# Five turns instead of three for the first two token chunks, with the partial sums added in the output by accumulating DMAs

## The chip, the cores and the metric

The kernel runs on one core of one Trainium2 chip. The metric is the device time of one execution in microseconds (us). A core has five engines that this text speaks of: the tensor engine (PE in the profile, its weight loads PEld), the vector engine (DVE), the scalar engine (ACT), GpSimd (POOL) and the sync engine (SP), which here only issues DMAs.

## What is computed

Linear attention with softmaxed queries and keys, and behind it a feed-forward layer with h - tanh(h) as its activation:

```python
q_s = softmax(q, axis=-1)                 # q, k, v: (8 batches, 8 heads, 576 tokens, 64), float32
k_s = softmax(k, axis=2)                  # over the tokens
kv  = einsum('bhsd,bhse->bhde', k_s, v)
x   = einsum('bhsd,bhde->bhse', q_s, kv)  # then as (4608 tokens, 512)
h   = x @ w_in                            # w_in (512, 2048), float64
g   = h - tanh(h)
out = g @ w_out                           # w_out (2048, 512), float64; out in float32
```

## The kernel before

**Chunks and steps.** The 4608 tokens are nine chunks (j) of 512, each of four tiles of 128. The 2048 columns of the hidden layer are 16 slices (f) of 128. One step (j, f) has two products. `h_step` (L493) makes a slice of h, transposed, in 12 matmuls of 128x512 into the tile `ph`; two buffers of `ph` take turns. Each float32 operand is a sum of two float32r parts (`xh`, `xl` of x.T; two parts of each weight), and three of the four partial products are taken, so that four blocks of 128 rows make 12 matmuls. Behind it ACT and DVE work out g: `u`, `t`, `vv`, `m` on ACT (L503 to L511), and on DVE four instructions (L507, L512, L513, L514). ACT rounds g to `gh` (L516), POOL makes the rest `gl` (L519). `o_step` (L533) multiplies g of one step by a slice of w_out, 12 matmuls for the four tiles, into four PSUM banks `po`. It runs LAG = 2 steps behind its `h_step`: PE's order is h(n), o(n-2), h(n+1), o(n-1), and so on.

**Weights.** They come as float64, in 32 pieces of 128x512 (16 of w_in, 16 of w_out; 512 KB each). `load_weight` (L87) issues the DMA on SP, two pieces ahead of the decoding. `split_weight` (L100) decodes a piece into two float32r parts with integer and float work: for a common piece two ACT instructions (L125, L128), three on DVE (L135, L140, L145), one more on ACT (L153) and one on POOL (L154); a third of the pieces (`apart`) has one ACT and one POOL instruction more (L122, L123, L151) and one less on DVE (L132, L145). The intermediate `c` has three buffers in the pool `dec`, tag `c`.

**Preparing a chunk.** `prepare` (L444) makes x of a chunk: for each new batch it loads keys and values, takes the maximum of the keys over the tokens on DVE (`kv_max`) and PE, the exponentials (`kv_sub`: L272 on DVE, L273 on ACT), the products `pk` of keys and values (`kv_mm`, L284), and normed blocks `kvbd` of them (`kv_norm`, L297 to L302). Queries get maximum, difference (POOL, L366), exponential (ACT, L371), sum (DVE, L379) in `q_soft`, their quotient `qn` on POOL (L403) and a transpose `pt` on PE in `q_t`, and `x_mm` (L435) makes `px`, from which ACT and DVE write `xh` and `xl` (L440, L441). Each of these calls is put at a half step: the first half of a step stands behind its h product, the second behind its o product. `half_step` (L669) maps the places of `prepare` to half steps of the whole program, with maps of their own for chunks 1, 2 and 3. From chunk 2 on, the second part of a batch's values goes through the one buffer of tag `v`: POOL's memset (L194) waits until `pk` of the first part has read it, and then SP loads. Queries have one buffer of tag `q`; a load waits for the quotient of the tile before it.

**The order.** PE and SP take their work in program order (`manual_schedule`, L681); on DVE, ACT and POOL the Tile scheduler sets the order. Steps are numbered from 0. Steps 0 to 7 are chunk 0 with slices 0 to 7 (F0 = 8), steps 8 to 23 all of chunk 1, steps 24 to 31 the rest of chunk 0, and from step 32 on chunks 2 to 8 follow in order. At the end of the first turn of chunk 0 (its o product is in step 9) ACT copies the four banks (L555) and SP writes them to a place in DRAM (`aside`, L566); four steps before the end of the second turn they are loaded again (`o_back`), and DVE adds them to the banks (L558), which SP then writes to the output. All other chunks end with four copies (L564), on ACT but for the last chunk's, into the tag `c`, and SP's writes (L569). Four pieces of the weights are decoded ahead of step 0, 13 in steps 0 to 7, and 15 in steps 8 to 19, five in four steps.

Of the kernel before, what the change touches and what calls it, by code (L numbers as in the profile page):

```python
# [19 lines left out]
# h - tanh(h) = h*u*C2*((u + PA)**2 + PB), u = h*h, to float32's last bits for u <= U_MAX.  # L20
U_MAX = 0.04
# (M_SCALE*h)**2 as an integer is 0 up to there.
# [5 lines left out]
# 2**-112 times the largest high word of a float64 that float32 can hold, read as a float32.  # L28
# [4 lines left out]
def attn_moe_kernel(  # L33
# [46 lines left out]
    # A piece of the weights, 128 x 512, arrives as float64 in the place where its two  # L80
    # float32r parts stay.
# [5 lines left out]
    def load_weight(kind: str, f: int):  # L87
        # What the second chunk's attention loads goes ahead of the pieces that can wait.
# [11 lines left out]
    def split_weight(kind: str, f: int, *after):  # L100
        """Decode a piece behind the instructions in after; other work may come at a yield."""
# [14 lines left out]
        # The exponent's eight lowest-order usable bits move into float32's field by a product  # L116
        # with 2**-112 on the word read as a float32 and a shift by three. The low word gives
        # the three bits that are missing: its first three, rounded, where 15/16 keeps them
        # under eight.
# [39 lines left out]
    # Partition p of a pair of tiles has two tokens that follow one another, 2p and 2p + 1.  # L159
# [25 lines left out]
    def v_load(b: int, st: dict, u: int):  # L185
        # A one before the first token's values of a head, and one behind the second's.
# [33 lines left out]
    def kv_max_t(b: int, st: dict):  # L220
# [5 lines left out]
        # In two parts of 12 bits, which hold a float32.  # L226
# [502 lines left out]
```

## Time and profile before

| | |
|---|---|
| time, median of 3 runs | 944.33 us (944.32 to 944.75) |
| span of the profiled execution | 944.0 us, 12627 instructions |
| PE busy | 898.7 us, 95% |
| DVE busy | 637.2 us, 68% |
| ACT busy | 560.6 us, 59% |
| POOL busy | 350.6 us, 37% |
| mean granted TensorE clock | 0.987 |

The span is the time from the first to the last instruction of one profiled execution on its core; it lies 0.3 us under the median of the timed runs. A busy share is the time in which an engine had an instruction running. Rows of the timeline give the start from the beginning of the span, how long the row took, engine, line, operation, the tile written and those read, how many instructions are merged into the row, and, in square brackets, the idle time of that engine just before it and what ended it. Rows of the windows give, for a stretch A:B, its length and then busy time and number of instructions of PE, PEld, DVE, ACT and POOL, the granted clock, the DMA share and GB/s.

### The profile page before, as it was taken

How to read it: one execution, taken by the hardware profiler on the slowest of the kernel's cores; microseconds unless marked ns; L12 is line 12 of the kernel's file. 1: busy time of each engine (PE TensorE's matmuls, PEld its weight loads, DVE VectorE, ACT ScalarE, POOL GpSimd, SP SyncE). 2: the span in 40 equal slices, each digit the busy share in tenths (PEclk: the TensorE clock that was granted, in tenths of full speed). 3: DMA queues.
4: the chain of work that ended last, by engine and by line, in shares of the span. 5: the costliest groups of instructions: out<-in, count | busy, mean ns of one | idle time of the engine just before them, and what ended most of it. 6: DMA issues, size and time to landing. Idle time of an engine off the chain costs nothing.

```text
span 944.0 us, 12627 instructions
## 1 busy us (share of the span) xinstructions
PE 898.7 (95%) x4676; PEld 738.0 (78%) x4676; DVE 637.2 (68%) x906; ACT 560.6 (59%) x976; POOL 350.6 (37%) x288
## 2 busy tenths in 40 slices
PE   6586998899999999999999999999999999999998
PEld 6365776678887888888888888888888888888886
DVE  6899989986658675856585747655765456444544
ACT  3677886765646556645564556545745565556554
POOL 4457576653224432432252224322433223222221
PEclk9888999999999999999999999999999999999999
DMA  9950084003032311150015001040210020001001
GB/s 265 300 193 0 1 286 94 0 23 122 14 96 50 87 37 45 34 123 1 12 57 123 1 1 57 23 101 1 68 45 1 1 68 13 1 1 45 1 1 45
DMA packets 79774, 57.44 MB, mean 61 GB/s; under 512 B 14688, under 2 KB 72032, under 8 KB 79712
## 3 DMA queue, kind: packets, MB, share of 16 engines
q1 hardware_dynamic: 79712, 56.63, 21.5%
q8 instruction: 37, 0.61, 0.3%
q14 instruction: 25, 0.20, 0.1%
HBM read 46.14 MB, written 10.49 MB: 60 GB/s over the span
## 4 chain that ended last, share of the span: by engine, by line
PE 79%; DVE 10%; ACT 4%; issue 4%; DMA 2%; POOL 1%; SPq 1%; DVEq 0%; POOLq 0%; ACTq 0%
PE po L542 36%; PE ph L499 35%; PE px L435 3%; PE pk L284 2%; DMA q<-in_q_dram 2%; PE pt L413 1%; DVE g L513 1%; DVE g L514 1%; DVE t L512 1%; DVE g L507 1%; DVE c_o L140 1%; DVE c_o L145 1%; DVE raw_o L135 1%; ACT gh L516 1%; ACT u L503 1%
## 5 line engine op out<-in xcount | busy, mean ns | idle before, releaser
L542 PE MATMUL po<-w_o,gh 128*128 128x512 f32 x1152 | 361.9, 395 | 0.0
L519 POOL TENSOR_TENSOR gl<-g,gh 128x512 fp32r<-128x512 f32 x143 | 196.2, 1372 | 435.5 <-ACT gh L516 408.0
L499 PE MATMUL ph<-xh,w_i 128*128 128x512 f32 x1152 | 315.0, 395 | 4.3 <-ACT xh L440 2.1
L499 PEld LDWEIGHTS ph<-xh,w_i 128*128 128x128 f32 x1152 | 214.0, 189 | 50.3 <-ACT xh L440 2.8
L507 DVE SCALAR_TENSOR_TENSOR g<-u,ph 128x512 f32<-128x512 f32 x144 | 98.4, 683 | 229.4 <-ACT t L505 227.3
L542 PEld LDWEIGHTS po<-w_o,gh 128*128 128x128 f32 x1152 | 214.7, 189 | 44.6 <-ACT aside L555 0.4
L542 PE MATMUL po<-w_o,gl 128*128 128x512 f32 x576 | 227.1, 394 | 7.4 <-POOL gl L519 7.3
L516 ACT CAST gh<-g 128x512 fp32r<-128x512 f32 x144 | 89.4, 621 | 196.4 <-DVE g L514 189.5
L499 PE MATMUL ph<-xl,w_i 128*128 128x512 f32 x576 | 155.8, 392 | 2.5 <-DVE xl L441 2.5
L503 ACT ACTIVATE u<-ph 128x512 f32<-128x512 f32 x144 | 85.8, 596 | 93.5 <-PE ph L499 93.1
L513 DVE SCALAR_TENSOR_TENSOR g<-vv,g 128x512 f32<-128x512 f32 x144 | 121.2, 842 | 22.7 <-ACT vv L509 12.5
L542 PEld LDWEIGHTS po<-w_o,gl 128*128 128x128 f32 x576 | 108.6, 189 | 34.6 <-POOL gl L519 10.8
L499 PEld LDWEIGHTS ph<-xl,w_i 128*128 128x128 f32 x576 | 108.6, 189 | 27.0 <-DVE xl L441 3.4
L514 DVE COPY_PREDICATED g<-m,t 128x512 f32<-128x512 int32 x144 | 118.6, 823 | 3.4
L509 ACT ACTIVATE vv<-u,b_pa 128x512 f32<-128x512 f32 x144 | 104.9, 728 | 1.7 <-DVE g L513 1.7
L511 ACT ACTIVATE m<-ph 128x512 int32<-128x512 f32 x144 | 86.5, 601 | 21.3 <-DVE g L507 21.0
L512 DVE TENSOR_TENSOR t<-ph,t 128x512 f32<-128x512 f32 x144 | 98.0, 681 | 1.4 <-ACT m L511 1.1
L505 ACT ACTIVATE t<-ph 128x512 f32<-128x512 f32 x144 | 85.3, 592 | 0.0
L435 PE MATMUL px<-qs,kvbd 128*128 128x128 f32 (+1 forms) x304 | 41.0, 281 | 8.7 <-DVE kvbd L302 7.1
L435 PEld LDWEIGHTS px<-qs,kvbd 128*128 128x128 f32 x304 | 39.3, 195 | 12.7 <-ACT t L505 7.5
L366 POOL TENSOR_TENSOR q<-q,mq 128x1024 f32<-128x1024 f32 x15 | 30.0, 2003 | 37.5 <-DVE mq L365 37.4
L403 POOL TENSOR_TENSOR qn<-q,sq 128x512 f32<-128x512 f32 x30 | 33.6, 1120 | 18.3 <-DVE sq L381 18.1
(101 smaller groups left out, 637.7 us busy)
## 6 DMA issues: line engine op xcount, KB each, us to landing
k<-in_k_dram SPq DMA_DIRECT2D x16, 512.0 KB, 5.6
raw_i<-in_moe_w_in_dram SPq DMA_DIRECT2D x16, 512.0 KB, 8.3
raw_o<-in_moe_w_out_dram SPq DMA_DIRECT2D x16, 512.0 KB, 9.7
q<-in_q_dram SPq DMA_DIRECT2D x15, 512.0 KB, 4.3
v<-in_v_dram SPq DMA_DIRECT2D x14, 512.0 KB, 5.8
out_dram<-o SPq DMA_DIRECT2D x28, 256.0 KB, 2.0
kr<-in_k_dram SPq DMA_DIRECT2D x8, 128.0 KB, 6.3
spare_v<-in_v_dram SPq DMA_DIRECT2D x2, 512.0 KB, 7.8
```

The costliest lines, as they stand in the source:

```text
L435: nc.tensor.matmul(px[:, a, p0:p1], kvbd[b % 2][:, a, :], qs[:, a, p0:p1], start=True, stop=True)
L499: nc.tensor.matmul(ph, w[:, i, c], x[:, c, :], start=(n == 0), stop=(n == len(ops) - 1))
L503: nc.scalar.activation(u, ph, AF.Square)
L507: nc.vector.scalar_tensor_tensor(g, u, C2, ph, op0=ALU.mult, op1=ALU.mult)
L509: nc.scalar.activation(vv, u, AF.Square, bias=b_pa)
L511: last = nc.scalar.activation(m, ph, AF.Square, scale=M_SCALE)
L512: nc.vector.tensor_tensor(t, ph, t, op=ALU.subtract)
L513: nc.vector.scalar_tensor_tensor(g, vv, PB, g, op0=ALU.add, op1=ALU.mult)
L514: nc.vector.copy_predicated(g, m, t)
L516: nc.scalar.copy(gh, g)
L519: eng.tensor_tensor(gl, g, gh.bitcast(F32), op=ALU.subtract)
L542: nc.tensor.matmul(po[t], g[:, cols], wt["o", f][:, w], start=(begin and n == 0), stop=(end and n == 2),)
```

## The change

The first two chunks take the weights in five turns instead of three: steps 0 to 3 are chunk 0 with slices 0 to 3, steps 4 to 11 chunk 1 with slices 0 to 7, steps 12 to 19 chunk 0 with 4 to 11, steps 20 to 27 chunk 1 with 8 to 15, steps 28 to 31 chunk 0 with 12 to 15. From step 32 on the steps are as before. Five pieces of the weights are decoded in steps 0 to 3, and then one in each step, from 4 to 26. Chunk 1 is prepared in steps 0 to 3 instead of 0 to 7, and chunk 2's tiles are spread over the half steps from 55 on, seven for every 17 places of `prepare`, instead of from 48 on, 12 for every 15. `kv_norm` stands ahead of the first product that reads its blocks.

Each turn ends with ACT's copies of the four banks into the tag `c` (20 copies for the two chunks, where there were eight, and four additions on DVE). The first turn of a chunk is written to the output by SP. The sums of a later turn are added to what stands in the output by a DMA with `accum_op=ALU.add`, issued by POOL: twelve such DMAs of 256 KB, four each for the turns that end with steps 19, 27 and 31. `aside`, `o_back` and the additions are gone.

```diff
-        for b in new:
-            put(km + 3, lambda: kv_norm(b, st))
...
+            if new & {b for b, _, _ in batches(i)} and not normed:
+                normed = True
+                put(km + 3, lambda: kv_norm(b, st))
             put(at, lambda i=i: x_mm(i))
...
-    def o_step(j: int, f: int):
+    def o_step(n: int):
+        j, f = steps[n]
         gh, gl = gs.pop((j, f))
-        begin = f == 0 or (j == 0 and f == F0)
-        end = f == NF - 1 or (j == 0 and f == F0 - 1)
+        begin = n == 0 or steps[n - 1] != (j, f - 1)
+        end = n == len(steps) - 1 or steps[n + 1] != (j, f + 1)
...
-            if j == 0 and f < NF - 1:
-                if t % 2 == 0:
-                    both = ap.tile([P, 2, DM], F32, name=f"aside{t}", tag="k", bufs=NKP)
-                o = both[:, t % 2]
-                nc.scalar.copy(o, po[t])
-            elif j == 0:
-                o = back[t // 2][:, t % 2]
-                nc.vector.tensor_tensor(o, po[t], o, op=ALU.add)
-            elif j == NCH - 1 and t % 2:
+            if j == NCH - 1 and t % 2:
                 o = gp.tile([P, DM], F32, name=f"o{j}_{f}_{t}", tag="g")
                 nc.vector.tensor_copy(o, po[t])
             else:
                 o = dec.tile([P, DM], F32, name=f"o{j}_{f}_{t}", tag="c")
                 nc.scalar.copy(o, po[t])
-            if f < NF - 1:
-                nc.sync.dma_start(aside[t], o)
-            else:
-                for rows, p0, p1 in rows_of(out, j * TPC + t):
+            for rows, p0, p1 in rows_of(out, j * TPC + t):
+                if (j, t) in written:
+                    nc.gpsimd.dma_start(rows, o[p0:p1], accum_op=ALU.add)
+                else:
                     nc.sync.dma_start(rows, o[p0:p1])
+            written.add((j, t))
...
-    F0 = 8
-    BACK = 4
-    steps = [(0, f) for f in range(F0)] + [(1, f) for f in range(NF)]
-    steps += [(0, f) for f in range(F0, NF)]
+    turns = [(0, 0, 4), (1, 0, 8), (0, 4, 12), (1, 8, 16), (0, 12, 16)]
+    steps = [(j, f) for j, f0, f1 in turns for f in range(f0, f1)]
+    F0 = turns[0][2]
+    BOTH = len(steps)
...
-            begin = 2 * (NF + F0)
-            return begin - 9 + at if at < 9 else begin + (at - 9) * 12 // 15
+            begin = 2 * (BOTH - turns[-1][2] + turns[-1][1]) - 1
+            return begin - 9 + at if at < 9 else begin + (at - 9) * 7 // 17
...
-            elif n < F0 + SPREAD:
-                pieces_upto(THEN + -(-(len(pieces) - THEN) * (n + 1 - F0) // SPREAD), last)
-            if n == 2 * NF - BACK:
-                o_back()
+            elif split < len(pieces):
+                pieces_upto(split + 1, last)
```

Three places show how the order moves. The first is PE behind the products `pk` of batch 1's keys and values; `pt` are transposed queries and `px` the products that give chunk 1's x. Before, from the second `pk` on:

```order
L284 MATMUL pk_574<-spare_v_431,k_1_416 64x65 x16
L284 MATMUL pk_574<-vr_423,kr_418 64x65 x8
L413 MATMUL pt_690<-ident,qn_688 128x128 x4
L499 MATMUL ph_4_704<-xh_289,w_i_499 128x512 x4
L499 MATMUL ph_4_704<-xl_290,w_i_499 128x512 x4
L499 MATMUL ph_4_704<-xh_289,w_i_499 128x512 x4
L435 MATMUL px_759<-qs_695,kvbd_94 128x128 x4
L542 MATMUL po_0_0_558<-w_o_488,gh_2_543 128x512 x2
```

And PE of the changed kernel from the same `pk` on (its lines are numbered otherwise: L501 is the h product, L535 the o product):

```order
L284 MATMUL pk_503<-spare_v_454,k_1_413 64x65 x16
L284 MATMUL pk_503<-vr_420,kr_415 64x65 x8
L413 MATMUL pt_554<-ident,qn_552 128x128 x4
L435 MATMUL px_570<-qs_559,kvbd_94 128x128 x4
L413 MATMUL pt_579<-ident,qn_577 128x128 x4
L501 MATMUL ph_2_594<-xh_286,w_i_354 128x512 x4
L501 MATMUL ph_2_594<-xl_287,w_i_354 128x512 x4
L501 MATMUL ph_2_594<-xh_286,w_i_354 128x512 x4
L435 MATMUL px_635<-qs_584,kvbd_94 128x128 x4
L413 MATMUL pt_644<-ident,qn_642 128x128 x4
L535 MATMUL po_0_0_651<-w_o_343,gh_0_385 128x512 x2
```

The first `px` stood behind the h product of step 4 and stands now ahead of that of step 2, and the four tiles take one half step each instead of one step each.

The second place is PE at the products `pk` of batch 2's keys and values, in chunk 0's last turn, before:

```order
L284 MATMUL pk_2015<-v_0_1697,k_0_1691 64x65 x16
L542 MATMUL po_0_0_1174<-w_o_1676,gh_15_1906 128x512 x2
L542 MATMUL po_0_0_1174<-w_o_1676,gl_15_1908 128x512
L542 MATMUL po_0_1_1178<-w_o_1676,gh_15_1906 128x512 x2
L542 MATMUL po_0_1_1178<-w_o_1676,gl_15_1908 128x512
L542 MATMUL po_0_2_1182<-w_o_1676,gh_15_1906 128x512 x2
L542 MATMUL po_0_2_1182<-w_o_1676,gl_15_1908 128x512
L542 MATMUL po_0_3_1186<-w_o_1676,gh_15_1906 128x512 x2
L542 MATMUL po_0_3_1186<-w_o_1676,gl_15_1908 128x512
L499 MATMUL ph_10_2059<-xh_289,w_i_1108 128x512 x4
L499 MATMUL ph_10_2059<-xl_290,w_i_1108 128x512 x4
L499 MATMUL ph_10_2059<-xh_289,w_i_1108 128x512 x4
```

Behind these rows the second `pk` follows, which reads `v_1`. In the changed kernel:

```order
L284 MATMUL pk_2172<-v_0_1852,k_0_1846 64x65 x16
L535 MATMUL po_8_0_1789<-w_o_1989,gh_14_2043 128x512 x2
L535 MATMUL po_8_0_1789<-w_o_1989,gl_14_2045 128x512
L535 MATMUL po_8_1_1793<-w_o_1989,gh_14_2043 128x512 x2
L535 MATMUL po_8_1_1793<-w_o_1989,gl_14_2045 128x512
L535 MATMUL po_8_2_1797<-w_o_1989,gh_14_2043 128x512 x2
L535 MATMUL po_8_2_1797<-w_o_1989,gl_14_2045 128x512
L535 MATMUL po_8_3_1801<-w_o_1989,gh_14_2043 128x512 x2
L535 MATMUL po_8_3_1801<-w_o_1989,gl_14_2045 128x512
L284 MATMUL pk_2172<-v_1_2189,k_1_1848 64x65 x16
L284 MATMUL pk_2172<-vr_1855,kr_1850 64x65 x8
L413 MATMUL pt_2230<-ident,qn_2228 128x128 x4
```

Between the two `pk` stood an o and an h product; now there is the o product alone.

The third place is ACT in step 33, at the end of chunk 0's last turn. Before, no copy stood there, since DVE added the banks:

```order
L503 ACTIVATE u_1_2463<-ph_1_2450 128x512
L505 ACTIVATE t_1_2465<-ph_1_2450 128x512
L509 ACTIVATE vv_1_2469<-u_1_2463,b_pa 128x512
L511 ACTIVATE m_1_2471<-ph_1_2450 128x512
L503 ACTIVATE u_2_2513<-ph_2_2500 128x512
```

In the changed kernel:

```order
L507 ACTIVATE t_1_2492<-ph_1_2477 128x512
L549 COPY o_15_0_2510<-po_12_0_2370 128x512
L511 ACTIVATE vv_1_2496<-u_1_2490,b_pa 128x512
L549 COPY o_15_1_2516<-po_12_1_2374 128x512
L513 ACTIVATE m_1_2498<-ph_1_2477 128x512
L549 COPY o_15_2_2522<-po_12_2_2378 128x512
L549 COPY o_15_3_2528<-po_12_3_2382 128x512
L518 CAST gh_1_2503<-g_1_2494 128x512
L505 ACTIVATE u_2_2544<-ph_2_2531 128x512
```

Four copies stand among the work on g. The tag `c` has three buffers, so the fourth copy waits for the accumulating DMA of the first, and `gh` of step 33 is queued behind it.

More of the change, by code (lines that the diff above doesn't have):

```diff
@@ L476, in prepare @@
             put(km + 3, lambda: kv_mm(b, st, NKP))
-        unit = None
+        unit, normed = None, False
         for i, at in when.items():
@@ L484, in prepare @@
             put(at - 3, lambda i=i: q_t(i))
+            if new & {b for b, _, _ in batches(i)} and not normed:
+                normed = True
+                put(km + 3, lambda: kv_norm(b, st))
             put(at, lambda i=i: x_mm(i))
-        for b in new:
-            put(km + 3, lambda: kv_norm(b, st))
     gs = {}
     po = {}
+    written = set()
     def h_step(j: int, f: int):
@@ L521, in h_step @@
         return last
-    dram = ctx.enter_context(tc.tile_pool(name="dram", bufs=1, space=bass.MemoryType.DRAM))
-    aside = dram.tile([TPC, P, DM], F32, name="aside")
-    back = []
-    def o_back():
-        for n in range(2):
-            t = ap.tile([P, 2, DM], F32, name=f"back{n}", tag="k", bufs=NKP)
-            nc.sync.dma_start(t, aside[2 * n : 2 * n + 2].rearrange("t p m -> p t m"))
-            back.append(t)
-    def o_step(j: int, f: int):
+    def o_step(n: int):
+        j, f = steps[n]
         gh, gl = gs.pop((j, f))
-        begin = f == 0 or (j == 0 and f == F0)
-        end = f == NF - 1 or (j == 0 and f == F0 - 1)
+        begin = n == 0 or steps[n - 1] != (j, f - 1)
+        end = n == len(steps) - 1 or steps[n + 1] != (j, f + 1)
         for t in range(TPC):
@@ L540, in o_step @@
             cols = slice(t * P, (t + 1) * P)
-            for n, (g, w) in enumerate(((gh, 0), (gh, 1), (gl, 0))):
+            for m, (g, w) in enumerate(((gh, 0), (gh, 1), (gl, 0))):
                 nc.tensor.matmul(
@@ L545, in o_step @@
                     wt["o", f][:, w],
-                    start=(begin and n == 0),
-                    stop=(end and n == 2),
+                    start=(begin and m == 0),
+                    stop=(end and m == 2),
                 )
@@ L564, in o_step @@
                 nc.scalar.copy(o, po[t])
-            if f < NF - 1:
-                nc.sync.dma_start(aside[t], o)
-            else:
-                for rows, p0, p1 in rows_of(out, j * TPC + t):
+            for rows, p0, p1 in rows_of(out, j * TPC + t):
+                if (j, t) in written:
+                    nc.gpsimd.dma_start(rows, o[p0:p1], accum_op=ALU.add)
+                else:
                     nc.sync.dma_start(rows, o[p0:p1])
+            written.add((j, t))
     LAG = 2
-    F0 = 8
-    BACK = 4
-    steps = [(0, f) for f in range(F0)] + [(1, f) for f in range(NF)]
-    steps += [(0, f) for f in range(F0, NF)]
+    turns = [(0, 0, 4), (1, 0, 8), (0, 4, 12), (1, 8, 16), (0, 12, 16)]
+    steps = [(j, f) for j, f0, f1 in turns for f in range(f0, f1)]
+    F0 = turns[0][2]
+    BOTH = len(steps)
     steps += [(j, f) for j in range(2, NCH) for f in range(NF)]
-    FIRST, THEN, SPREAD = 4, 2 * F0 + 1, 12
+    FIRST, THEN = 4, 2 * F0 + 1
     APART = range(6, 2 * NF, 3)
@@ L685, in attn_moe_kernel @@
                 pieces_upto(FIRST + -(-(THEN - FIRST) * (n + 1) // F0), last)
-            elif n < F0 + SPREAD:
-                pieces_upto(THEN + -(-(len(pieces) - THEN) * (n + 1 - F0) // SPREAD), last)
-            if n == 2 * NF - BACK:
-                o_back()
+            elif split < len(pieces):
+                pieces_upto(split + 1, last)
             for half in range(2):
                 if half and n >= LAG:
-                    o_step(*steps[n - LAG])
+                    o_step(n - LAG)
                 for call in calls.pop(2 * n + half, ()):
@@ L695, in attn_moe_kernel @@
         for n in range(len(steps) - LAG, len(steps)):
-            o_step(*steps[n])
+            o_step(n)
 _INS = ["q", "k", "v", "moe_w_in", "moe_w_out"]
```

## The prediction

> **What bounds the kernel now.** I read the slices of the page first, then the windows by stage, then PE's timeline. In the slices (23.6 us each) PE is short of full in the first nine, and there DVE is the fullest engine:
>
> ```profile
> PE   6586998899999999999999999999999999999998
> ...
> DVE  6899989986658675856585747655765456444544
> ...
> PEclk9888999999999999999999999999999999999999
> ```
>
> PE's timeline gives the first h products of steps 0, 8, 24, 32 and 33, and of steps 128 and 143 in the last chunk:
>
> ```profile
> 31.04 1.19 PE L499 MATMUL ph<-xh,w_i 128*128 128x512 f32 x4 [1.67 <-ACT xh L440]
> ...
> 78.75 2.05 PE L435 MATMUL px<-qs,kvbd 128*128 128x128 f32 x8 [7.12 <-DVE kvbd L302]
> ...
> 106.88 1.21 PE L499 MATMUL ph<-xh,w_i 128*128 128x512 f32 x4 [0.47 <-ACT xh L440]
> ...
> 210.85 1.07 PE L499 MATMUL ph<-xh,w_i 128*128 128x512 f32 x4
> ...
> 263.61 1.08 PE L499 MATMUL ph<-xh,w_i 128*128 128x512 f32 x4
> ...
> 269.08 1.08 PE L499 MATMUL ph<-xh,w_i 128*128 128x512 f32 x4
> ...
> 848.02 1.08 PE L499 MATMUL ph<-xh,w_i 128*128 128x512 f32 x4
> ...
> 930.08 1.08 PE L499 MATMUL ph<-xh,w_i 128*128 128x512 f32 x4
> ```
>
> A step of PE work alone is 269.08 - 263.61 = 5.47 us, 2.74 for each product. A chunk is (848.02 - 263.61) / 6 = 97.4, so preparing one costs PE 97.4 - 16 x 5.47 = 9.9. From step 0 to step 32 there are 32 h products, 30 o products and two preparations: 62 x 2.735 + 19.8 = 189.4 us of work, and it took 263.61 - 31.04 = 232.6. So 43 us are lost there, and all the change does lies there. The windows say to whom (columns: stretch, length, busy us and instructions of PE, PEld, DVE, ACT, POOL, clock):
>
> ```profile
> 37.77:106.88 69.11, 51.00 (x289) 40.07 (x287) 67.21 (x84) 50.41 (x89) 43.19 (x31) 0.88 0.33 114
> 106.88:210.85 103.97, 94.34 (x394) 73.44 (x395) 94.98 (x123) 78.64 (x142) 67.38 (x44) 0.98 0.31 91
> 140.00:180.00 40.00, 34.47 (x138) 26.29 (x138) 39.67 (x52) 29.96 (x55) 25.70 (x16) 0.96 0.33 71
> 210.85:263.61 52.76, 52.76 (x325) 44.10 (x324) 32.78 (x51) 31.17 (x55) 17.15 (x17) 1.00 0.19 61
> ```
>
> DVE is busy 67.21 of 69.11 us until step 8 and 39.67 of 40.00 in the worst of the decoding, and then 20 us idle in the last eight steps, where PE runs full. So DVE bounds the first 200 us, and idles where its work is gone. Part of its time is not its own: the same instruction takes 1.76 us beside POOL's and 0.68 without:
>
> ```profile
> 69.16 1.76 DVE L140 SCALAR_TENSOR_TENSOR c_o<-raw_o 128x512 uint32<-128x512 uint32 x1
> ...
> 96.48 0.68 DVE L140 SCALAR_TENSOR_TENSOR c_i<-raw_i 128x512 uint32<-128x512 uint32 x1
> ...
> 68.60 1.77 POOL L154 TENSOR_TENSOR w_i<-c_i,w_i 128x512 fp32r<-128x512 f32 x1
> ```
>
> **The change part by part.** DVE's work from 37.77 (its first instruction on g, with the same order ahead of it in both kernels) to step 32 is 67.21 + 94.98 + 32.78 = 195.0 us. The change takes none of it away; by its order four instructions for batch 3's maximum come ahead of step 32, 4 x 0.80 = 3.2, which makes 198.2. What changes is where DVE has to wait.
>
> *Steps 0 to 3.* Ahead of chunk 1's first h product stand 48 DVE instructions from 37.77 on, where before 84 started in that stretch. At 67.21 / 84 = 0.80 us each that is 38.4. Twice DVE must wait for PE, since h of steps 2 and 3 now stands behind a `px`: a transpose (0.35), h (2.74) and two ACT instructions (0.6 each) less the copies of x that DVE and ACT do meanwhile (0.6 and 0.7), 3.0, and much the same for step 3, 2.5. So step 4 starts at 37.77 + 38.4 + 5.5 = 81.7. If POOL disturbs less it is 79, if the waits add up 85. By then PE has done 4 h, 2 o and a preparation, 26.3 us of work; before, that much was done at about 86. The 7.12 us wait for `kvbd` goes; what is late next is h of step 2 behind `px`.
>
> *Steps 4 to 27.* What is left for DVE is 198.2 - 38.4 less the 32 instructions that stand in steps 28 to 31 at 32.78 / 51 = 0.64, 20.6: 139.2 us. PE needs 24 x 5.47 and about a third of a preparation, 3.4: 134.7. One piece a step makes the two nearly equal, so neither runs far ahead. DVE's idle share here lies between that of the densest stretch, 0.33 of 40 us, and that of steps 8 to 23, 9.0 of 104. I take 2%, since DVE stays the longer one: 2.8 (0 to 12). DVE is done with step 27 at 81.7 + 139.2 + 2.8 = 223.7. PE is about level with it: in the decoding a step's last DVE instruction ends 4.5 us behind its h product (160.85 to 165.36),
>
> ```profile
> 160.85 0.61 PE L542 MATMUL po<-w_o,gh 128*128 128x512 f32 x2
> ...
> 164.62 0.74 DVE L514 COPY_PREDICATED g<-m,t 128x512 f32<-128x512 int32 x1
> ```
>
> and PE does an o product and a `px` meanwhile, 4.2. Step 28 starts at 223.4.
>
> *Steps 28 to 31.* Here chunk 2's tiles are pressed from eight steps into four. PE's work is 21.9 + 9.9 - 3.4 = 28.4. Three chains no longer fit beside it. Their links before:
>
> ```profile
> 220.93 1.15 PE L284 MATMUL pk<-v,k 128*64 128x65 f32 x32
> ...
> 222.63 0.12 POOL L194 MEMSET v<- 128x16 f32 x1
> 222.78 0.38 SPq L196 DMA_DIRECT2D v<-in_v_dram  x1
> ...
> 227.68 1.15 PE L284 MATMUL pk<-v,k 128*64 128x65 f32 x32
> 228.76 0.68 PE L284 MATMUL pk<-vr,kr 64*64 64x65 f32 x16
> ...
> 230.65 0.40 SPq L351 DMA_DIRECT2D q<-in_q_dram  x1
> ...
> 232.72 0.86 DVE L302 TENSOR_TENSOR kvbd<-pk,rs 64x256 f32<-64x256 f32 x2
> ...
> 234.97 1.22 DVE L365 TENSOR_REDUCE mq<-q 128x16 f32<-128x1024 f32 x1 [1.40 <-DMA q<-in_q_dram]
> ...
> 242.80 1.05 POOL L403 TENSOR_TENSOR qn<-q,sq 128x512 f32<-128x512 f32 x1 [4.57 <-DVE sq L381]
> ```
>
> The second `pk` waits for values loaded only when the first `pk` has been read: memset, issue and a lone load of 4.3 us (230.65 to 234.97, where DVE waited for it), 4.6 in all. An o and an h product hid it; now there is one of 2.74. That leaves 1.9, and up to 3 more when the memset stands behind a late `gl` on POOL: 3.0. Then `px` waits for `kvbd`, 4.2 us behind the last `pk` (229.4 to 233.6), beside 3.1 of PE work: 1.1. And the quotient for the last tile came 15.0 us behind the second `pk` (228.8 to 243.85); PE's work up to its transpose is 11.3 and the 1.1 just counted: 2.6 more. Sum 28.4 + 6.7 = 35.1: step 32 at 258.5.
>
> *Ends of turns.* Copies on ACT are more by 12 x 0.6, hidden, since ACT is busy 78.64 of 104. Where decoding goes on they stand among ACT's work as `aside` did, whose copies came over four microseconds and cost PE nothing to speak of (0.08 us over its usual pace):
>
> ```profile
> 119.47 0.58 ACT L555 COPY aside<-po 128x512 f32<-128x512 f32 x1
> ...
> 123.63 0.61 ACT L555 COPY aside<-po 128x512 f32<-128x512 f32 x1
> ...
> 124.29 0.73 PE L542 MATMUL po<-w_o,gh 128*128 128x512 f32 x2
> ```
>
> No row shows an accumulating DMA or POOL's issue of one. It must read what it adds to and then write, so it costs at least a write, 2.0 us, and, with all else in its way, up to the longest median here, 9.7:
>
> ```profile
> raw_o<-in_moe_w_out_dram SPq DMA_DIRECT2D x16, 512.0 KB, 9.7
> ...
> out_dram<-o SPq DMA_DIRECT2D x28, 256.0 KB, 2.0
> ...
> q_rest<-in_q_dram SPq DMA_DIRECT2D x8, 128.0 KB, 3.1
> ```
>
> I take a read and a write in turn, 3.1 + 2.0 = 5.1, and 1 us for the issue (POOL's shortest row of this size above is 1.05). In step 33 the first copy ends 1.3 us behind h; 6.1 us later the fourth copy may start, and is done at 7.9. PE wants that bank at 2.74 + 2.74 + 2.06 = 7.5: 0.4 lost. At the end of the turn of step 19 the third copy waits in the same way, some 1.5 us beyond PE's need, half of it hidden behind DVE; at that of step 27 two preparation products more cover it. Together 1.2. POOL's gl is queued behind these issues, with over 4 us until o reads it.
>
> The Trainium skill, "DMA: Bandwidth & Descriptors" (section "Anatomy of one DMA — SWDGE (gpsimd) path"), fits a GpSimd-issued transfer as 2.0 us and its bytes at 436 GB/s, which for 256 KB would be 2.6 us by estimate, for plain copies. By that the 1.2 us of this term would be nothing, and the forecast 939.2. No run here shows such a transfer yet.
>
> **The sum.** Step 32 moves from 263.6 to 258.5, and 1.2 is lost behind that: a gain of 3.9 us on a span of 944.0. Beyond step 33 the order is the same. The span is 0.3 under the median, so the time is 944.3 - 3.9 = 940.4.
>
> **The rivals.** *DVE stays full* (0.2): PE falls behind nowhere, DVE idles 1% in steps 4 to 27 and the loads come early enough. Then only its gaps count, 4 in the first steps, 1.4, and 9 in the last four: 37.77 + 198.2 + 14.4 = 250.4, a gain of 13 and 931. For it speaks 39.67 of 40.00; against it that two engines with equal work never fit without gaps.
>
> *The gain is given back* (0.17): the first turn saves its 4 us, and the chains of steps 28 to 31 take 10 to 11 instead of 6.7, for instance because `gl` of step 27 comes 3 us late and the clock falls after the wait, as it did around the 7.12 us wait (the 0.88 of that window). Then 944.3 within 1.9 us, which is 0.2%, about what the measurement can tell from no change.
>
> *Slower, by the accumulating DMAs* (0.21): ACT stands still before the third or fourth copy, and behind it wait `gh`, and so `gl` and PE. The price is one for one beyond what the cover allows at each of three ends; from about 7 us a transfer instead of 5.1, 2 us at each end and in all 6, nothing is left of the 3.9 and it turns to loss. At the bound of 9.7 us it is 4.6 at each, 14 in all, some of it hidden: 950. For it speaks that three banks of `c` serve four copies; against it the 2.0 us of a write. The Trainium skill, in the same page, section "SWDGE vs HWDGE vs iDMA", says that GpSimd writes the descriptors into SBUF, where DVE can lock it out. That would lengthen the issue where DVE is busiest, and work for this rival; no run here shows it yet.
>
> **How the numbers follow.** Forecast (935 to 942.4) 0.42, more gain 0.2, no difference 0.17, slower 0.21. Faster by over 0.2% is 0.42 + 0.2 = 0.62. The low end takes in the DVE rival, 931. The high end takes the accumulating rival up to its middle, 949, and leaves the worst of it and an even shorter first part outside.
>
> **What would show it.** Right: step 4 at 79 to 85 us without a long wait for `kvbd`; DVE over 95% from there to about 220, with PE waits for `gl` of less than a microsecond; waits of PE ahead of the second `pk` of batch 2 and of the last tile's transpose, 2 to 5 us each; step 32 at 254 to 263; accumulating DMAs that land in 4 to 7 us. Wrong: PE waits for `po` banks at the ends of turns, ACT idle ahead of a copy for a DMA, or DVE idle by more than a tenth in steps 4 to 27.

## The result and the profile after

The changed kernel takes 955.0 us in the median of four runs (953.57 to 956.11), against 944.54 for the kernel before on the same chip (944.32 to 944.79). The ratio is 1.0111, with a 95% interval of 1.0097 to 1.0126: about 10.5 us slower, where 3.9 us less was forecast. Each run takes 1.8 us more than its span; the profiled one has a span of 953.5, against 944.0 before.

The same three slices of the page as before (23.6 to 23.8 us each):

```profile
PE   7579999889799999999999999999999999999998
...
DVE  6967777869556675767575757755766547544544
...
PEclk9679999889999999999999999999999999999999
```

PE is at nine tenths or more in slices 4 to 7, where before it had 6, 9, 9 and 8, while DVE is at seven tenths there (before, eight and nine). Then PE drops in slices 8, 9 and 11, and the clock in 8 and 9 too. PE's timeline says when steps 0, 4, 20, 28 and 32 begin:

```profile
30.67 1.19 PE L501 MATMUL ph<-xh,w_i 128*128 128x512 f32 x4 [1.67 <-ACT xh L440]
...
79.80 1.10 PE L501 MATMUL ph<-xh,w_i 128*128 128x512 f32 x4
...
172.93 1.07 PE L501 MATMUL ph<-xh,w_i 128*128 128x512 f32 x4
...
235.43 1.18 PE L501 MATMUL ph<-xh,w_i 128*128 128x512 f32 x4
...
274.35 1.08 PE L501 MATMUL ph<-xh,w_i 128*128 128x512 f32 x4
```

Before, steps 20, 28 and 32 began at 184.2, 238.9 and 263.6. So the changed kernel is 11.2 us ahead at step 20, 3.4 ahead at step 28 and 10.7 behind at step 32. It gets 1.2 back at step 38 and keeps 9.5 to the end. The windows between these points (columns as before):

```profile
30.67:79.80 49.13, 34.69 (x213) 28.44 (x214) 37.98 (x58) 30.19 (x52) 22.98 (x19) 0.72 0.32 94
79.80:172.93 93.13, 89.01 (x386) 71.70 (x384) 73.09 (x107) 75.09 (x138) 50.53 (x35) 1.00 0.51 151
172.93:235.43 62.50, 53.69 (x219) 41.51 (x218) 51.43 (x68) 44.32 (x79) 39.91 (x29) 0.92 0.19 37
235.43:274.35 38.92, 32.61 (x215) 26.99 (x214) 24.22 (x39) 18.95 (x34) 15.68 (x16) 0.91 0.47 102
```

In steps 4 to 19 PE works 89.0 of 93.1 us and DVE only 73.1. DVE waits there for PE's products, by way of ACT's `t`, which reads them. This is the instruction that opens each step's work on g, with its count, busy us, mean ns, idle us before it and what ended that:

```profile
L509 DVE SCALAR_TENSOR_TENSOR g<-u,ph 128x512 f32<-128x512 f32 x15 | 10.3, 687 | 15.2 <-ACT t L507 13.6 <-POOL c_o L151 1.6
```

So PE is the bound there. Where the lead goes again, the timelines show three kinds of wait. The first are copies at the ends of turns (in steps 6 and 22; 1.9 us more in step 14):

```profile
97.30 0.74 PE L535 MATMUL po<-w_o,gh 128*128 128x512 f32 x2 [2.11 <-ACT o L549]
...
198.24 0.59 ACT L549 COPY o<-po 128x512 f32<-128x512 f32 x1 [0.97 <-DMA out_dram<-o]
...
198.87 0.94 PE L535 MATMUL po<-w_o,gh 128*128 128x512 f32 x2 [2.50 <-ACT o L549]
```

The second kind comes around step 20. The rest of the queries is issued only at 167.5 us, behind ten weight pieces and a batch's keys and values, which themselves follow the writes of an end of a turn on SP, and it lands late; DVE waits, POOL waits for DVE with `gl` behind it, and PE for `gl`. One step on, PE waits for a piece that is decoded just in time:

```profile
167.54 1.27 SPq L340 DMA_DIRECT2D q_rest<-in_q_dram  x2
...
174.63 0.69 DVE L365 TENSOR_REDUCE mq_rest<-q_rest 128x8 f32<-128x512 f32 x1 [1.77 <-DMA q_rest<-in_q_dram]
...
175.39 1.43 POOL L366 TENSOR_TENSOR q_rest<-q_rest,mq_rest 128x512 f32<-128x512 f32 x1 [5.22 <-DVE mq_rest L365]
...
178.56 0.66 PE L535 MATMUL po<-w_o,gl 128*128 128x512 f32 x1 [1.10 <-POOL gl L521]
...
187.90 0.50 PE L535 MATMUL po<-w_o,gh 128*128 128x512 f32 x1 [1.22 <-POOL w_o L154]
```

The third kind stands in steps 28 to 31: the lone loads of values and queries, and the quotient for the last tile. (The profile calls what ended the first of these waits "issue"; that it is the load of values is shown below, where the load is left out and the wait goes.)

```profile
246.41 1.52 PE L284 MATMUL pk<-v,k 128*64 128x65 f32 x32 [3.94 <-issue]
...
254.36 1.22 DVE L365 TENSOR_REDUCE mq<-q 128x16 f32<-128x1024 f32 x1 [3.86 <-DMA q<-in_q_dram]
...
263.11 0.66 PE L413 MATMUL pt<-ident,qn 128*128 128x128 f32 x4 [2.36 <-POOL qn L403]
```

And the operation that no row of before showed, POOL's accumulating DMA (duration of an issue, then landing, min/median/max):

```profile
L553 POOL DMA_DIRECT2D out_dram<-o x12: 856/891/1531, 193.7 to 289.8; - x12
...
DMA to landing us min/median/max: 3.7/4.6/6.2
```

Eight of these twelve belong to the turns that end with steps 27 and 31, and PE waits for no copy at either end.

### The profile page after: what moved, and what is told of

Its sections match the earlier page's. It is cut to its first block, busy times and chain, and to the rows that moved or that the text cites. A ratio compares the mean times of both kernels' runs of the same rounds, so it can differ in the third digit from the quotient of the medians.

```text
span 953.5 us, 12685 instructions
## 1 busy us (share of the span) xinstructions
PE 906.4 (95%) x4676; PEld 746.7 (78%) x4676; DVE 618.2 (65%) x902; ACT 567.0 (59%) x988; POOL 354.4 (37%) x300
## 4 chain that ended last, share of the span: by engine, by line
PE 80%; DVE 7%; DMA 4%; ACT 4%; issue 3%; POOL 1%; SPq 0%; DVEq 0%; ACTq 0%; POOLq 0%
PE po L535 36%; PE ph L501 36%; PE px L435 3%; PE pk L284 2%; PE pt L413 2%; DMA k<-in_k_dram 1%; DMA q<-in_q_dram 1%; DVE t L514 1%; DVE g L515 1%; DVE g L516 1%; DMA q_rest<-in_q_dram 1%; ACT u L505 1%; ACT gh L518 1%; ACT vv L511 1%; DVE g L509 1%
## 5 line engine op out<-in xcount | busy, mean ns | idle before, releaser
L535 PE MATMUL po<-w_o,gh 128*128 128x512 f32 x1152 | 364.6, 398 | 9.6 <-ACT o L549 6.7
L501 PE MATMUL ph<-xh,w_i 128*128 128x512 f32 x1152 | 317.0, 397 | 1.7 <-ACT xh L440 1.7
L535 PEld LDWEIGHTS po<-w_o,gh 128*128 128x128 f32 x1152 | 215.5, 190 | 58.3 <-ACT o L549 10.1
L509 DVE SCALAR_TENSOR_TENSOR g<-u,ph 128x512 f32<-128x512 f32 x144 | 98.6, 685 | 248.1 <-ACT t L507 244.4
L501 PEld LDWEIGHTS ph<-xh,w_i 128*128 128x128 f32 x1152 | 216.9, 191 | 46.8 <-ACT xh L440 1.9
L535 PE MATMUL po<-w_o,gl 128*128 128x512 f32 x576 | 227.7, 395 | 1.6 <-POOL gl L521 1.6
L501 PE MATMUL ph<-xl,w_i 128*128 128x512 f32 x576 | 156.8, 394 | 1.1 <-DVE xl L441 1.1
L515 DVE SCALAR_TENSOR_TENSOR g<-vv,g 128x512 f32<-128x512 f32 x144 | 118.4, 822 | 23.4 <-ACT vv L511 12.4
L535 PEld LDWEIGHTS po<-w_o,gl 128*128 128x128 f32 x576 | 109.3, 190 | 26.7 <-POOL gl L521 2.4
L501 PEld LDWEIGHTS ph<-xl,w_i 128*128 128x128 f32 x576 | 109.4, 190 | 25.5 <-DVE xl L441 1.6
L516 DVE COPY_PREDICATED g<-m,t 128x512 f32<-128x512 int32 x144 | 116.3, 808 | 3.3
L514 DVE TENSOR_TENSOR t<-ph,t 128x512 f32<-128x512 f32 x144 | 98.1, 681 | 3.2 <-ACT m L513 2.6
L435 PEld LDWEIGHTS px<-qs,kvbd 128*128 128x128 f32 x304 | 39.4, 195 | 7.2 <-issue 3.2
```

Source lines behind the costliest of these rows:

```text
L435: nc.tensor.matmul(px[:, a, p0:p1], kvbd[b % 2][:, a, :], qs[:, a, p0:p1], start=True, stop=True)
L501: nc.tensor.matmul(ph, w[:, i, c], x[:, c, :], start=(n == 0), stop=(n == len(ops) - 1))
L509: nc.vector.scalar_tensor_tensor(g, u, C2, ph, op0=ALU.mult, op1=ALU.mult)
L514: nc.vector.tensor_tensor(t, ph, t, op=ALU.subtract)
L515: nc.vector.scalar_tensor_tensor(g, vv, PB, g, op0=ALU.add, op1=ALU.mult)
L516: nc.vector.copy_predicated(g, m, t)
```

## The experiments

Each experiment was forecast before it ran, and five theories were set against each other. **A**: the order of turns leaves chunk 2's preparation four steps. **B**: the accumulating DMAs cost by themselves. **C**: chunk 2's first loads stand behind the writes of a turn's end on SP's queue and come late. **D**: the copies wait for places that they share with the decoding. **E**: DVE's work is bunched in steps 20 to 28 and takes any lead of PE back. Ratios are against the kernel before on the same chip, with their intervals. For the main ones, the starts of steps in the profiled execution:

| kernel | median us | ratio (95%) | step 20 | step 28 | step 32 |
|---|---|---|---|---|---|
| before | 944.5 | 1 | 184.2 | 238.9 | 263.6 |
| changed | 955.0 | 1.0111 (1.0097 to 1.0126) | 172.9 | 235.4 | 274.4 |
| e9: copies in weight places | 948.45 | 1.0037 (1.0023 to 1.0052) | 170.2 | 228.2 | 267.6 |
| e14: e9 without the lone loads | 941.23 | 0.9960 (0.9946 to 0.9974) | 171.0 | 231.0 | 260.2 |
| e17: e9, lone loads earlier | 944.75 | 1.0011 (1.0002 to 1.0019) | 170.4 | 230.1 | 263.5 |
| e12: eight steps last, loads early | 944.03 | 0.9995 (0.9986 to 1.0005) | 179.1 | 238.0 | 263.3 |
| e15: three turns, twelve steps last | 957.67 | 1.0142 (1.0127 to 1.0157) | 197.0 | 254.2 | 276.9 |

### Turns, transfers and loads, one at a time

The first experiment (e1) changes the order of turns and the pace of decoding, and takes chunk 2's spacing from before:

```
-    turns = [(0, 0, 4), (1, 0, 8), (0, 4, 12), (1, 8, 16), (0, 12, 16)]
+    turns = [(0, 0, 4), (1, 0, 8), (0, 4, 8), (1, 8, 16), (0, 8, 16)]
+    FIRST, THEN, SPREAD = 4, 2 * F0 + 1, 20
-                pieces_upto(split + 1, last)
+                pieces_upto(min(len(pieces), THEN + -(-(len(pieces) - THEN) * (n + 1 - F0) // SPREAD)), last)
-            begin = 2 * (BOTH - turns[-1][2] + turns[-1][1]) - 1
+            begin = 2 * (BOTH - turns[-1][2] + turns[-1][1])
```

> Third turn cut to four steps and last turn lengthened to eight (chunk 0 f4-7, chunk 1 f8-15, chunk 0 f8-15), the 23 pieces left spread over 20 steps, chunk 2's tiles at the old spacing over eight steps. All twelve accumulating DMAs stay. Theory A (the order of turns: chunk 1 ends with step 27, so chunk 2's preparation gets four steps where it had eight, and PE stands there): step 4 at 79.8 as measured, 20 steps of 5.47 and some 6 us of ends of turns until step 24 at 195, then 53 us as before from step 24 to 32: step 32 at 248 to 252, time 930 to 934. Theory B (the accumulating DMAs hold the copies and PE at each end): the three ends stay, 950 or more. Theory C (chunk 2's first loads come late because they stand behind the writes on SP's queue): the loads still stand behind them, 940 to 950.

It took 954.27 us (1.0102, 1.0087 to 1.0117). A missed and B's number was met, and PE's timeline says why: the waits for copies had grown to 17 us. The two longest stand behind the third end, in step 18:

```profile
174.16 1.22 PE L535 MATMUL po<-w_o,gh 128*128 128x512 f32 x2 [2.79 <-ACT o L549]
182.55 1.22 PE L535 MATMUL po<-w_o,gh 128*128 128x512 f32 x2 [6.75 <-ACT o L549]
```

The second (e2) takes the old order of turns with the sums added in the output, so that only how and where the sums are kept differs from before (and `kv_norm`'s place):

```
+    turns = [(0, 0, 8), (1, 0, 16), (0, 8, 16)]
+    FIRST, THEN, SPREAD = 4, 2 * F0 + 1, 12
```

> The old order of turns (eight steps, sixteen, eight) and the old pace of decoding, with the sums added in the output by four accumulating DMAs instead of aside, back and the additions on VectorE. Theory A: as before but for the loads back and the additions, whose step before took 7.5 us against 6.3 in the changed kernel: 942 to 944. Theory B: the four accumulating DMAs cost some 2 to 5 us at their end: 946 to 949. Theory C: 944, as before.

947.28 us (1.0028, 1.0016 to 1.0040), slower than before and within B's range. But B's place is wrong: its accumulating DMAs come at step 33, and PE waits at the end of the first turn, which SP writes with plain DMAs:

```profile
122.56 0.73 PE L535 MATMUL po<-w_o,gh 128*128 128x512 f32 x2 [1.95 <-ACT o L549]
126.12 1.22 PE L535 MATMUL po<-w_o,gh 128*128 128x512 f32 x2 [2.59 <-ACT o L549]
```

This gave theory D. At the same place before, the copies stood in tag `k` and PE lost nothing.

The third (e3) puts chunk 2's first loads ahead on SP's queue:

```
+            if at == 0:
+                return 24
```

> The changed kernel with chunk 2's first loads (keys, first values, the rest of the queries) put at step 12, ahead of the write of the second turn's end on SP's queue. Theory C: VectorE no longer waits 1.8 us for the queries and GpSimd 5 us behind it, steps 20 to 22 take 11 us instead of 19, time 946 to 949. Theories A and B: those steps lose as much to the decoding itself, 953 to 955.

952.62 us (1.0082, 1.0058 to 1.0105), between the two expectations, with an interval that overlaps the changed kernel's. Steps 20 and 21 became full steps, but step 20 began 4.5 us later than in the changed kernel (177.5 against 172.9), with chunk 2's maximum now among the decoding, and step 22 took 11.3 us, with PE waiting 3.4 for a copy: other waits took over.

The fourth (e4) takes the accumulating DMAs out:

```
-                    nc.gpsimd.dma_start(rows, o[p0:p1], accum_op=ALU.add)
+                    pass
```

> The changed kernel with the twelve accumulating DMAs left out (so three of the five partial sums never reach the output). Theory B: with no transfer to wait for, the ends of turns cost nothing and the time is 942 to 946. Theory A: only the 2.7 us that PE waits for copies at step 22 and what the clock loses behind it go, 950 to 953. Theory C: 953 to 955.

949.41 us (1.0045, 1.0028 to 1.0062), 5.6 us less than the changed kernel. The time lies below A's range and above B's. That alone cannot tell the transfer from the place it holds, since without it a copy's place is free at once.

### The copies' places

The edit for the next three puts the copies of the first three ends where before had `aside`:

```
+                if n < 20:
+                    if t % 2 == 0:
+                        both = ap.tile([P, 2, DM], F32, name=f"o{j}_{f}_{t}", tag="k", bufs=NKP)
+                    o = both[:, t % 2]
+                else:
                     o = dec.tile([P, DM], F32, name=f"o{j}_{f}_{t}", tag="c")
```

> The changed kernel with the copies of the first three ends of turns in the four places of tag k (where the kernel before had aside), not in the three of c that the decoding uses too; all twelve accumulating DMAs stay. Theory D (the copies wait for places that they share with the decoding, and the transfers only for as long as they hold such a place): PE's waits for copies (6.4 us at three ends) and the clock lost behind them go, 944 to 948, as without the DMAs or below. Theory B (the accumulating DMAs themselves, their issue on GpSimd and their traffic): only the two ends that write gain, 951 to 953.

> The order of turns of the first experiment (last turn of eight steps) and the copies of the first three ends in tag k. Theories A and D together: the 16 us that PE waited for copies there go, step 32 at 250 to 256, time 931 to 937. If the last turn's length is worth nothing (A falls): as the changed kernel with tag k, 944 to 948. Theory B: 945 to 952, since eight of the transfers still come while PE needs the banks.

> The old order of turns with the sums added in the output (second experiment), and the copies of the end during decoding in tag k, as the kernel before had them. Theory D: PE's 4.5 us of waits at that end go, 942 to 944. Theory B: no change from the second experiment, 946 to 948, because there the accumulating transfers come only at the last end.

The old order of turns (e7) took 943.39 us (0.9985, 0.9976 to 0.9995), 3.9 us less than the second experiment by this edit alone: D held, with plain writes and no accumulating DMA near. The changed kernel with `k` (e5) took 952.81 (1.0084, 1.0064 to 1.0104) and the other order (e6) 949.51 (1.0049, 1.0032 to 1.0066): D's numbers were missed in both, and B's met. Yet PE's waits for copies were down to 0.7 and 3.6 us, but the places in `k` are those of chunk 2's keys, whose load now stood behind the transfers, and DVE waited for it in front of its work on g, 2.7 us in e5. In e6, in step 19:

```profile
177.47 0.69 DVE L213 TENSOR_TENSOR km<-k 128x512 f32<-128x512 f32 x1 [6.61 <-DMA k<-in_k_dram]
```

So the edit had its own fault, and B was not yet out. The cleaner test takes other places: those of the two `w_out` pieces that are loaded last (e9; e11 with the first experiment's turns, e10 and e12 with the third's early loads as well).

```
+                if n < 20:
+                    if t % 2 == 0:
+                        tag = f"wo{NF - 1 - t // 2}"
+                        both = wts.tile([P, 2, DM], F32, name=f"o{j}_{f}_{t}", tag=tag)
+                    o = both[:, t % 2]
```

> The changed kernel with the copies of the first three ends of turns in the places of two weight pieces that are loaded last (o pieces 14 and 15): nothing else uses these places then, neither the decoding nor chunk 2's keys, which VectorE had to wait for in the variant with tag k. Theory D (places): PE's 6.4 us at the three ends go and no new wait for keys comes, step 20 near 169, step 24 near 196, 944 to 948. Theory E (VectorE's work for decoding and chunk 2 is bunched in steps 20 to 28, and the last turn is too short; a lead of PE is taken back there): step 24 near 196, but step 32 at 271 to 273 as in the other variants, 950 to 953.

> The same, and chunk 2's first loads at step 12. Theories C and D together: 941 to 945. Theory E: step 28 gains, the four steps behind it cost 37 to 42 us still: 947 to 951.

> The last turn of eight steps, and the copies of the first three ends in those weight places. Theories A and D: no wait for copies, none of 6.6 us for keys: step 24 at 203 to 208, step 32 at 256 to 261, 937 to 942. Theory E without its part on the last turn (VectorE bunched): step 24 at 212 to 218, step 32 at 266 to 271, 946 to 950.

> The same, and chunk 2's first loads at step 12, so that VectorE can take chunk 2's maxima early. Theories A, C and D: step 24 at 198 to 204, step 32 at 252 to 257, 932 to 938. Theory E: 943 to 948.

e9: 948.45 us, 6.5 less than the changed kernel, with all twelve accumulating DMAs in it, between D's range and E's and 0.45 from D's. The lead at step 20 is D's, and E is right that most of it is gone again by step 32. Its windows of steps 4 to 19, 20 to 27 and 28 to 31:

```profile
79.50:170.20 90.70, 88.71 (x385) 71.67 (x383) 76.04 (x107) 74.08 (x138) 52.45 (x35) 1.00 0.50 151
170.20:228.20 58.00, 50.42 (x218) 39.75 (x219) 52.60 (x69) 43.85 (x79) 43.51 (x29) 0.97 0.21 46
228.20:267.60 39.40, 32.68 (x215) 27.21 (x215) 24.45 (x39) 19.11 (x34) 15.67 (x16) 0.91 0.47 100
```

The early loads added nothing to it (e10: 950.11 us, 1.0053, 1.0034 to 1.0073, within E's range; C falls there). With eight steps for the last turn they did: e11 took 949.11 (1.0044, 1.0029 to 1.0059) and e12, with the loads early, 944.03, level with before, both in E's ranges of time. In e12 the last eight steps run at PE's pace, as A says, but A's time is missed, since steps 4 to 23 take 128.7 us in place of e9's 119.5:

```profile
208.50:263.30 54.80, 53.36 (x326) 44.05 (x325) 38.54 (x56) 31.61 (x59) 25.74 (x23) 1.00 0.36 73
```

Then the accumulating DMAs once more, out of e9 (e13):

> The variant with the copies in weight places (948.5 us), and the twelve accumulating DMAs left out (three of five partial sums never reach the output). Theory B (the transfers cost by themselves: GpSimd's 0.9 us issues, their traffic): 943 to 946. Theory D (they cost only by the places they hold): 947 to 949.

946.86 us (1.0024, 1.0012 to 1.0036). That is 1.6 us less than e9, between the two expectations, and the intervals overlap: theory B's price lies between nothing and some 3 us for all twelve.

### The short last turn

One lone load out of the changed kernel (e8; the first tile of values serves twice):

```
     def v_load(b: int, st: dict, u: int):
+        if b == 2 and u == 1:
+            return
...
+        if b == 2 and u == 0:
+            st["v", 1] = vt
```

> The changed kernel without the load of batch 2's second half of values (the first half is used twice, so that batch's result is another). It prices the lone load in the short last turn: PE's 3.9 us ahead of the second pk and what the clock loses behind it. If that wait is on the path: 949 to 951. If the chains behind it (the quotient for the last tile) end late anyway: 953 to 955.

953.61 us (1.0093, 1.0078 to 1.0109). PE's wait ahead of the second `pk` went, but the one for the last tile's quotient grew from 2.36 to 4.48 us: two chains side by side, and one alone is worth 1.4. So both were taken out of e9 (e14), the load in `q_load` likewise:

```
     def q_soft(unit):
+        if unit == (2, 1):
+            qs_of[unit] = qs_of[2, 0]
+            return
```

> The variant with the copies in weight places, without the load of batch 2's second half of values and without load, maximum, exponential and sum of its second half of queries (the first halves are used twice there). If the two lone loads and the chain behind the second make the last turn long: PE's waits of 3.9 and 2.8 us, VectorE's 4.0 us for the queries and the clock lost behind them go, steps 28 to 32 in 29 to 32 us instead of 39.4, time 938 to 942. If it is PE's clock or the work itself: 945 to 948.

941.23 us (0.9960, 0.9946 to 0.9974), 7.2 us under e9: steps 28 to 31 in 29.2 us, PE busy throughout at full clock. This takes out work too (DVE has 19.0 us in that stretch instead of 24.4), so 7.2 us is an upper bound for the price of the waits.

```profile
230.97:260.20 29.23, 29.23 (x215) 24.46 (x214) 18.97 (x34) 17.76 (x33) 13.63 (x14) 1.00 0.52 100
```

With all work left in, the loads can only be issued earlier. In e17 the first `pk` stands one `px` and one h product earlier, and the second tile's transpose ahead of step 29's h product:

```
-            put(km, lambda: kv_mm(b, st, 0))
+            put(km - 1 if j == 2 else km, lambda: kv_mm(b, st, 0))
-            put(at - 3, lambda i=i: q_t(i))
+            put(15 if i == 2 * TPC + 2 else at - 3, lambda i=i: q_t(i))
```

(`v_load` of the second half moves with the first `pk`.) In e18, the load of the rest of the queries also goes to step 12:

```
-                    put(0 if j == 1 else max(0, at - 12), lambda unit=unit: q_load(unit))
+                    put(0 if j == 1 else -22 if unit[1] == "rest" and j == 2 else max(0, at - 12), lambda unit=unit: q_load(unit))
```

> The variant with the copies in weight places, all work left in, with the first pk of batch 2 ahead of the px of the rest tile (a step earlier, so that the second half of values loads beside an h product too) and the second tile's transpose moved ahead of step 29's h product (so that the second half of queries loads earlier). If the lone loads make the last turn long: step 28 to 32 in 32 to 35 us instead of 39.4, time 941 to 945. If they only uncover another chain as late: 946 to 949.

> The same, and the load of the rest of the queries alone at step 12, ahead of the write on SP's queue. If its late landing (VectorE 1.8 us, GpSimd 5 us, PE 2 us of waits for gl around step 20) is on the path: 2 to 4 us less than the variant beside it. If VectorE's work around step 20 is late anyway: the same within 1.5 us.

e17: 944.75 us, 3.7 under e9, with steps 28 to 31 in 33.4 us in place of 39.4, both within what was expected if the lone loads make the last turn long. Of these 6.0 us, 1.9 only moved ahead, since the first `pk` now stands before step 28, which begins that much later; step 32 comes 4.1 us earlier.

```profile
230.10:263.50 33.40, 29.93 (x182) 24.77 (x182) 21.20 (x36) 18.30 (x33) 15.96 (x16) 0.95 0.60 118
```

e18: 943.74 us (0.9987, 0.9978 to 0.9996), less than e17 by 1.0 us in the medians and by 2.3 in the ratios, whose intervals do not overlap: with chunk 2's keys left where they were, theory C's price is 1 to 2 us, between the two expectations. With the copies in weight places, these two edits take back what the change gives away, with all work left in, and no more: 0.9 us under before on the same chip is less than the 0.2% that the prediction took as no difference. e7 is no better a claim (1.2 us under).

### Fewer turns

If four steps are too few and eight are level, twelve should be better. Three turns, 23 pieces in 15 steps, one end during decoding, its copies in weight places (e15) or in `c` (e16):

```
+    turns = [(0, 0, 4), (1, 0, 16), (0, 4, 16)]
+    FIRST, THEN, SPREAD = 4, 2 * F0 + 1, 15
```

> Only three turns: chunk 0 f0-3, all of chunk 1, chunk 0 f4-15, the 23 pieces within 15 steps, chunk 2's tiles over the last twelve steps; the copies of the first end in weight places, those of the second (decoding is done) in c; four accumulating DMAs left, at the end. If the order of turns is what gives the gain away: VectorE full until step 20 at 172 to 180, then 12 steps and 9.9 us of preparation without long waits, step 32 at 249 to 257, time 930 to 938. If VectorE's sum of work decides wherever it stands: step 32 at 260 to 264, 941 to 945.

> The same with all copies in c. Theory D: only the first end is hit, 2 to 4 us, so 2 to 4 us above the variant beside it. If shared places matter little where only plain writes hold them: the same within 1 us.

957.67 and 960.40 us (1.0171, 1.0154 to 1.0189), the slowest of all. D was met (2.7 us between them); both expectations of e15 missed. Steps 4 to 19 took 116.7 us with DVE at 98%:

```profile
80.30:197.00 116.70, 99.61 (x395) 75.08 (x394) 114.40 (x138) 90.02 (x164) 71.50 (x49) 0.96 0.38 113
```

An instruction of DVE takes 0.83 us there (114.40 / 138), and 0.68 in the changed kernel's same steps (73.09 / 107). The decoding's two-input instruction L140 shows it most. First e15, then the changed kernel (columns: count, busy us, mean ns, idle before):

```profile
L140 DVE SCALAR_TENSOR_TENSOR c_o<-raw_o 128x512 uint32<-128x512 uint32 x8 | 10.5, 1313 | 0.1
L140 DVE SCALAR_TENSOR_TENSOR c_i<-raw_i 128x512 uint32<-128x512 uint32 x7 | 10.2, 1462 | 0.0
```

```profile
L140 DVE SCALAR_TENSOR_TENSOR c_o<-raw_o 128x512 uint32<-128x512 uint32 x6 | 4.1, 680 | 0.0
L140 DVE SCALAR_TENSOR_TENSOR c_i<-raw_i 128x512 uint32<-128x512 uint32 x4 | 2.7, 677 | 0.0
```

At a pace half as fast again (23 pieces in 15 steps, where the changed kernel decodes one in each) L140 costs twice as much; the prediction's row had it at 1.76 us beside POOL's work. It is not DVE as a whole that slows: L509 and L514, which read one operand from a PSUM bank (`ph`), take 0.68 to 0.69 us in both stretches, and L515, with both operands in SBUF, even fell from 0.98 to 0.86. The Trainium skill, "SBUF — State Buffer" (section "Who interferes with whom"), says that a DVE instruction with two inputs in SBUF contends with a GpSimd instruction that reads SBUF, and that whoever is second waits for the whole of the other. The durations of L140, and those of L509 and L514 beside it, agree with that, and L515's do not show it. POOL was busy 54% of the changed kernel's stretch and 61% of e15's, so its share alone does not tell the two apart, and no run here separates POOL's part from the rest.

## Why the prediction was wrong

By its own steps, on the spans (953.5 against a forecast of 940.1 there, 13.4 us):

- *Steps 0 to 3*: forecast 81.7 for step 4, measured 79.8, but by two errors that nearly cancel. The 48 DVE instructions were counted rightly, but they took 32.4 us and not 38.4, and DVE waited 9.5 us and not 5.5. So the near hit was luck in part, and the price of 0.80 us that fails in the next point was wrong here already:

```profile
37.94:79.80 41.86, 28.87 (x197) 24.42 (x198) 32.41 (x48) 26.91 (x46) 22.16 (x18) 0.75 0.21 70
```

- *Steps 4 to 27*: forecast 141.7 us, measured 155.6, 13.9 worse. This is the step that failed. It took DVE as the longer engine throughout, at the mean price of the dense decoding before, and spread its 139.2 us evenly. In truth DVE's work was 124.5 us (73.1 + 51.4, and 0.68 us an instruction in steps 4 to 19 in place of 0.80), less than PE's 142.7, so PE was the bound until step 20, which began about 3 us earlier than the forecast's even pace gives. Steps 20 to 27 took 62.5 us where the even pace gave 47. There PE waits 8.8 us: 2.7 for copies, 2.5 for `gh` and `gl`, 1.9 for a decoded piece, 1.7 for the diagonal `d` of chunk 2's maximum. It is busy 53.7 us at a granted clock of 0.92, by estimate 49.4 us of work at full clock and 4.3 lost. The sum had no such waits inside these steps, only an idle share of DVE.
- *Ends of turns*: "Where decoding goes on they stand among ACT's work as `aside` did" was false, and the term of 1.2 us was too small. `aside` stood in the four places of `k`; the new copies stand in the three of `c`, and the decoding holds these too. A copy waits for a piece, a piece for a copy's transfer, and PE for its bank. The two pairs e2 and e7, changed and e9, show it: 3.9 us for one end, 6.5 for three. Nearly all of it falls within the stretch of the point above. At the end of the last turn (step 33), where the sum has 0.4 lost, ACT's fourth copy does wait for the transfer of the first, but PE loses nothing.
- *Steps 28 to 31*: forecast 35.1, measured 38.9. The mechanism was right: second `pk` 3.9 us late (3.0 forecast), quotient 2.4 (2.6). Mis-sized was what stands behind a wait: at a granted clock of 0.91 PE is busy 32.6 us, where the same 215 instructions take 29.2 at full clock in e14. These 3.4 us were left out of the sum, though the rival by which the gain is given back named them: its chains of 10 to 11 us were right (38.9 - 28.4 = 10.5), and its time was missed by the point on steps 4 to 27. The work itself was 0.8 more than the 28.4 of the sum, and the wait for `kvbd` (1.1) did not come.
- *Behind step 32*: 1.2 us lost was forecast, 1.2 gained was measured. The changed kernel's step 37 took 6.3 us, before's 7.5. e7 has the same 6.3, with the old order of turns, so it goes with doing without the loads back and the additions.
- -1.9 + 13.9 + 3.8 - 2.4 = 13.4. The medians differ by 1.2 us more, since before's profiled span of 944.0, with the 1.8 us outside the span that every run here has, belongs to a time of 945.8, above its median.

The rival that forecast the loss, with a chance of 0.21, had one of its three ends right, that of the turn of step 19, and the wrong cause. It wanted transfers of 7 us or more, and they took 4.6, less than the 5.1 assumed; what a transfer costs here hangs on whether it holds one of three places for which the decoding asks as well (5.6 us between the changed kernel and e4, 1.6 or nothing to tell between e9 and e13). Its 950 left out the waits of steps 20 to 31 that are not for copies, and the clock. The Trainium skill's fit ("DMA: Bandwidth & Descriptors", "Anatomy of one DMA — SWDGE (gpsimd) path") made it 2.6 us by estimate, for plain copies; for an accumulating one the measurement decides, 3.7 to 6.2. Its warning that DVE can lock GpSimd's descriptor writing out ("SWDGE vs HWDGE vs iDMA") has no clear sign here: an issue took 0.89 us in the median and 1.53 at most.

All three of the prediction's signs of being wrong came: PE waited for banks at ends of turns, ACT stood idle ahead of a copy for a DMA, and DVE was idle a fifth of steps 4 to 27.

What is shown is the loss of 10.5 us: other places for the copies take back 6.5, earlier lone loads 3.7, and the load of the rest of the queries 1 to 2. What stays open is why the forecast's gain does not come with it: in e9, steps 20 to 27 still take 58.0 us, where PE is busy 50.4 and DVE 52.6. PE's waits there are for `gl`, for one decoded piece and for `d`, up to 2.6 us each. Issuing the loads earlier took back 1 to 2 us of them (e18); no run shows what the rest hangs on, or whether another order of DVE's work would free it. That DVE's work is bunched there is theory E, argued from these rows and tested by no run of its own.

## What to carry to other kernels

Before a copy, look which tag it goes to and who else takes places of it: here the price of a transfer was mostly the time for which it held a place that something else waited for, and plain writes were hit by it as accumulating ones were. Cost an engine by stage and not by its mean, and do not carry a mean price from one stage to another: DVE's ran from 0.68 us, spread out, to 0.83, pressed together, with a few lines at twice their price and others unchanged. When a stage's forecast is met, look whether its terms were met too. When a wait is taken out and the end does not move, look for the chain beside it before giving up the theory; here two had to go together.

## What was not expected of the hardware

Accumulating DMAs of 256 KB landed 3.7 to 6.2 us after their issue, plain ones by SP after 2.0 in the median, and an issue holds POOL for 0.9 us; all twelve together cost 1.6 us, or less than the measurement can tell, where the decoding's places are not shared. And the granted clock was 1.00 in the mean over the 93 us of steps 4 to 19, with a wait of 2.1 us and 1.9 us of waits near each other among them, but 0.92 and 0.91 in the two stretches behind, with waits of up to 3.9 us. In the last of them, waits of 6.3 us brought 3.4 us of slower work with them. Why some waits cost clock and others did not, no run here shows.
